# A two-part mixer: nine blocks of 512 tokens in place of sixteen half batches of 288, with TensorE's order written out

## The chip, the cores and the metric

The kernel runs on one core of one Trainium2 chip. The metric is the device time of one execution in microseconds (us). The kernel before takes 811.2 us, the median of three runs (810.45 to 811.35).

## What is computed

The reference has two parts, one behind the other. Chunked attention gives x; a mixer with two pairs of weight matrices follows, one pair across tokens and one across channels.

```python
B, H, S, D = 8, 8, 576, 64                # batches, heads, tokens, width of a head
# attention inside chunks of 64 tokens (9 chunks in each batch and head)
attn = softmax(q_c @ k_c.T / sqrt(D));  out = attn @ v_c
x = out as (B, S, 512)
# the mixer: w_tok1 576x256, w_tok2 256x576, w_ch1 512x1536, w_ch2 1536x512
xt = x.transpose(0, 2, 1)
u  = x + (relu(xt @ w_tok1) @ w_tok2).transpose(0, 2, 1)
out = u + relu(u @ w_ch1) @ w_ch2
```

The weights come as 64-bit floats, which the kernel turns into 32-bit ones itself. The sums over tokens stay inside one batch of 576 tokens. The channel part (the last line) treats each token by itself, so its tokens may be grouped across batches.

## The kernel before, in words

**Attention.** The tokens of the 8 batches are loaded as 36 tiles of 128 (L251, L256): tiles 0 to 4 hold batch 0 and the first 64 tokens of batch 1, tiles 5 to 8 the rest of batch 1, and so on. For a tile TensorE makes scores `s`; VectorE subtracts their maximum (`mx` L282, `pr` L285); ScalarE takes the exponential (L289). The probabilities then have to be transposed. In the first five tiles TensorE does that (L351, "t"); from tile 5 on VectorE transposes 32x32 blocks (L332), the result goes out to DRAM as `far` and comes back rearranged as `pf` (L337, L343), and ScalarE copies it to `pt` (L360). TensorE then makes `v`, VectorE divides into `x` (L400), ScalarE and GpSimd split x into a high part `xh` (L417) and a low part `xl` (L418). A product of two split operands takes three fp32r matmuls (high by high, low by high, high by low). x itself goes out and back through DRAM as `xt`, transposed, for the sum in u.

**Weights.** Each piece is fetched as raw 64-bit words (L139). ScalarE reads it twice (L156, L157), VectorE clamps, shifts, adds the sign and adds the low word (L160, L166, L173, L181), ScalarE rounds a high part (L225) and VectorE subtracts to get the low part (L231). Of the channel weights there are 24 pieces of 512 columns: c1 0 to 11 and c2 0 to 11. `convert(n)` puts the next n of VectorE's steps at a place in the program.

**Token part.** `tok1` (L476) gives for a batch two sums of 14 matmuls, 512 columns wide; `tok2` (L514) uses them for u, 288 tokens (half a batch) at a time. u is split into `uh` and `ul` (L524, L525). Batch 0 takes plain fp32 operands in one term in place of three (L485, L514).

**Channel part.** For a half batch and each of 12 pieces f, `ch1` (L535) does 12 matmuls of 288 columns; `gh` (L544, ScalarE) and `gl` (L545, VectorE) are made of the result; `ch2` (L575) does 12 more into four accumulators. Each ch2 stands one ch1 late, behind the ch1 of the next piece. At the end o is added up and written (L582 to L585).

**What sets the order.** The start (five tiles, tok1 and tok2 of batch 0) is written out by hand on TensorE, ScalarE and VectorE. Then, until batch 1's mixer begins, a scheduler places the instructions of all engines: both halves of batch 0 run through ch1 together, piece by piece, the second half keeps its g (L541) and runs ch2 afterwards, and the four tiles of batch 1 are spread over slots (`STARTS`, `JOBS`); the split of the token weights stands at the end of that (`split`). From batch 1 on TensorE's order is by hand; the other engines' comes from the scheduler. Each engine runs its instructions in its order, and so does SyncE with the DMAs: whoever waits holds up all behind it.

Of the kernel before, what the change touches and what calls it, by code (L numbers as in the profile page):

```python
# [8 lines left out]
F32 = mybir.dt.float32  # L9
# [41 lines left out]
X_BEFORE = ((), (), (0,), (1,), (2,), (3, 4))  # L51

END_FILL = (4, 3, 1)
STEP_FILL = (5, 5)

STARTS = ((8, 9, 11, 12), (13, 14, 16, 17), (18, 19, 21, 22), (23, 24, 26, 27))
STARTS = ((8, 9, 11, 12), (13, 14, 16, 17), (18, 19, 21, 22), (23, 24, 26, 27))
JOBS = [(9, "ready")]
JOBS += [(s, "part", j, k) for j, ss in enumerate(STARTS) for k, s in enumerate(ss)]
JOBS += [(27 + i, "split", i) for i in range(7)]  # L60


@with_exitstack
def attention_mixer_kernel(ctx, tc, qk_in, v_in, w1_in, w2_in, wc1_in, wc2_in, out):

# [36 lines left out]
    plan += [(("t2", k, n), w2_in, k * S + n * HALF, HALF) for n in range(2) for k in range(NT1)]  # L120
# [50 lines left out]
    def words_sign(i):  # L171
        ti = tops[i].bitcast(I32)
        nc.vector.scalar_tensor_tensor(  # L173
            out=ti, in0=raws[i][1][:, :, 1], scalar=-0x40000000, in1=ti,
            op0=ALU.bitwise_and, op1=ALU.bitwise_or,
        )
        raws[i][0].__exit__(None, None, None)
# [41 lines left out]
    def split_high(i):  # L219

        key, _, _, n = plan[i]
        name = "kept_" + "_".join(map(str, key))
        kept = ctx.enter_context(tc.tile_pool(name=name, bufs=1, reuse_waits="tile"))
        parts = tops[key, "parts"] = kept.tile([P, 2, n], F32R, name=name)
        nc.scalar.copy(out=parts[:, 0], in_=tops[i])  # L225
# [21 lines left out]
    xt = const.tile([P, S // BK, NDT, BK], F32, name="xt")  # L247
# [190 lines left out]
    def attn_x(b, i, ps=None):  # L438

        for t, rows, j in mix_tiles(b):  # L440
            if t != i:
                continue
            dst = xt[:, 4 * j:4 * j + (rows.stop - rows.start) // BK]
            if ps is None:
                far_in(tiles[t]["x"], dst, rows)
            else:
                nc.scalar.copy(  # L447
                    out=dst.rearrange("p i n c -> p n i c"),
                    in_=near(tiles[t]["x"], ps).rearrange("p (n q) -> p n q", n=NDT)[:, :, rows]
                    .rearrange("p n (i c) -> p n i c", c=BK),  # L450
                )
# [53 lines left out]
    def tok2(b, r, n, m, dst):  # L505

        uh, ul = dst
        ps = ps_acc.tile([P, 512], F32, tag="acc", name="ps_t2")
        for k in range(NT1):
            terms = [(r[k], tops["t2", k, n])] if b == 0 else [  # L510
                (r[k][ri], weights["t2", k, n][:, wi]) for wi, ri in THREE
            ]
            for q, (lhsT, rhs) in enumerate(terms):
                nc.tensor.matmul(  # L514
                    ps[:, :HALF], lhsT=lhsT[:, m * P:(m + 1) * P], rhs=rhs,
                    start=(k == 0 and q == 0), stop=(k == NT1 - 1 and q == len(terms) - 1),
                )
        u = pool.tile([P, HALF], F32, tag="u", name="u", bufs=4)
        nc.vector.tensor_tensor(  # L519
            out=u.rearrange("p (i c) -> p i c", c=BK),  # L520
            in0=ps[:, :HALF].rearrange("p (i c) -> p i c", c=BK),
            in1=xt[:, n * HALF // BK:(n + 1) * HALF // BK, m], op=ALU.add,
        )
        nc.scalar.copy(out=uh[:, m], in_=u)  # L524
        return lambda engine: engine.tensor_tensor(  # L525
            out=ul[:, m], in0=u, in1=uh[:, m].bitcast(F32), op=ALU.subtract
        )

    def ch1(u, f, kept=False):
        while ("c1", f) not in weights:  # L530
            convert(1)
        ps = ps_c1.tile([P, 512], F32, tag="c1", name="ps_c1")
        for k in range(NDT):
            for q, (wi, ui) in enumerate(THREE):
                nc.tensor.matmul(  # L535
                    ps[:, :HALF], lhsT=weights["c1", f][:, wi, k * P:(k + 1) * P], rhs=u[ui][:, k],
                    start=(k == 0 and q == 0), stop=(k == NDT - 1 and q == 2),
                )
# [11 lines left out]
    def g_parts():  # L550
# [8 lines left out]
    def ch2(b, n, u, f, g, accs):  # L559
# [13 lines left out]
        for e in range(NDT):  # L573
# [5 lines left out]
            if f < NFC - 1:  # L579
                continue  # L580
# [273 lines left out]
```

## Time and profile before

| | |
|---|---|
| median of three runs | 811.2 us |
| span of the profiled execution | 808.2 us |
| TensorE busy | 787.4 us, 97% |
| VectorE busy | 378.0 us, 47% |
| ScalarE busy | 240.7 us, 30% |
| GpSimd busy | 118.5 us, 15% |
| mean granted TensorE clock | 0.992 |

The page gives for the profiled execution its span alone, from the first instruction to the last; the median of the runs is 3.0 us above it, and that difference is what lies around the span. TensorE's share is an average of two stretches: in the first 180 us it is busy for 163.3, and from there until its last matmul it has no idle time that the profile shows. VectorE's 47% is an average too: it is busy for 49.9 of the 50 us from 52 to 102.

### The profile page before, as it was taken

The page shows a single profiled execution, that of the slowest core. Times are in us where ns is not written, and L with a number is a line of the kernel's source. Part 1 is how long each engine was busy: PE and PEld are TensorE (multiplying, and loading weights), DVE is VectorE, ACT ScalarE, POOL GpSimd, SP SyncE. Part 2 cuts the span into 40 slices and gives each one's busy share as a digit, 9 for nine tenths or more (in the row PEclk, how much of TensorE's full clock was granted, in tenths as well). Part 3 has the DMA queues.
Part 4 walks back from the last instruction along what each step waited for, and adds up shares of the span by engine and source line. Part 5 has one row for each costly group of instructions (what it writes and reads, how often), then busy time and mean ns, then how long its engine had stood idle before and what let it go on. Part 6 is the DMA issues. An engine that isn't in the chain of part 4 may idle for free.

```text
span 808.2 us, 17939 instructions
## 1 busy us (share of the span) xinstructions
PE 787.4 (97%) x7556; PEld 752.1 (93%) x7556; DVE 378.0 (47%) x799; ACT 240.7 (30%) x496; POOL 118.5 (15%) x137
## 2 busy tenths in 40 slices
PE   7889999899999999999999999999999999999997
PEld 5579989799999999999999999999999999999997
DVE  5989985545344344253534334344533445232111
ACT  4667643322232222132223222222223222121111
POOL 0000120401203021130203102030200302033000
PEclk8999999999999999999999999999999999999999
DMA  9953322344432233123441234222342223200000
GB/s 349 406 190 105 119 79 96 135 122 141 148 112 64 92 122 107 56 79 125 141 151 58 64 115 140 88 70 93 131 145 89 76 88 101 67 30 1 1 30 30
DMA packets 69985, 87.96 MB, mean 109 GB/s; under 512 B 8016, under 2 KB 48208, under 8 KB 69904
## 3 DMA queue, kind: packets, MB, share of 16 engines
q1 hardware_dynamic: 69904, 86.82, 32.5%
q8 instruction: 59, 0.97, 0.5%
q14 instruction: 22, 0.18, 0.1%
HBM read 59.92 MB, written 25.95 MB: 106 GB/s over the span
## 4 chain that ended last, share of the span: by engine, by line
PE 85%; DVE 8%; DMA 3%; ACT 2%; issue 1%; SPq 0%; ACTq 0%; DVEq 0%
PE acc L575 36%; PE ps_c L535 33%; PE ps_t L476 6%; PE ps_t L514 6%; PE ps_sv L309 2%; PE ps_sv L321 2%; DVE wtop L173 1%; DVE wtop L181 1%; DMA xc<-x 1%; DVE kept_c L231 1%; DVE wtop L160 1%; DMA raw_t<-in_w 1%; DMA pf<-far 1%; DVE wtop L166 1%; PE sum L485 0%
## 5 line engine op out<-in xcount | busy, mean ns | idle before, releaser
L535 PE MATMUL ps_c<-uh,kept_c 128*128 128x288 f32 x1536 | 310.8, 295 | 3.4 <-ACT xt L447 1.9
L575 PE MATMUL acc<-gh,kept_c 128*128 128x288 f32 x1536 | 311.9, 299 | 1.6 <-ACT kept_c L225 1.1
L535 PEld LDWEIGHTS ps_c<-uh,kept_c 128*128 128x128 f32 x1536 | 245.8, 188 | 4.8 <-ACT xt L447 2.1
L575 PEld LDWEIGHTS acc<-gh,kept_c 128*128 128x128 f32 x1536 | 244.2, 188 | 6.4 <-ACT kept_c L225 1.8
L535 PE MATMUL ps_c<-ul,kept_c 128*128 128x288 f32 x768 | 226.6, 295 | 0.0
L545 DVE SCALAR_TENSOR_TENSOR gl<-ps_c,gh 128x288 fp32r<-128x288 f32 x180 | 81.4, 452 | 310.1 <-ACT gh L544 309.9
L575 PE MATMUL acc<-gl,kept_c 128*128 128x288 f32 x768 | 219.5, 295 | 0.0
L544 ACT ACTIVATE gh<-ps_c 128x288 fp32r<-128x288 f32 x180 | 74.1, 411 | 317.1 <-PE ps_c L535 316.6
L535 PEld LDWEIGHTS ps_c<-ul,kept_c 128*128 128x128 f32 x768 | 144.2, 188 | 0.1
L575 PEld LDWEIGHTS acc<-gl,kept_c 128*128 128x128 f32 x768 | 142.9, 189 | 0.1
L418 POOL TENSOR_TENSOR xl<-x,xh 128x512 fp32r<-128x512 f32 x28 | 38.3, 1366 | 413.0 <-ACT xh L417 413.0
L584 POOL TENSOR_TENSOR o<-o,ul 128x288 f32<-128x288 f32 x56 | 44.1, 813 | 192.7 <-DVE o L582 191.1
L514 PE MATMUL ps_t<-kept_t,rh 128*128 128x288 f32 x224 | 44.7, 295 | 0.3 <-ACT rh L493 0.3
L289 ACT ACTIVATE pr<-pr 128x512 f32<-128x512 f32 x36 | 22.7, 632 | 61.6 <-DVE pr L285 59.9
L582 DVE TENSOR_TENSOR o<-acc,uh 128x288 f32<-128x288 f32 x56 | 22.7, 448 | 36.1 <-PE acc L575 31.5
L476 PE MATMUL ps_t<-xh,kept_t 128*128 128x512 f32 x112 | 36.0, 405 | 2.5 <-ACT xh L417 2.5
L524 ACT CAST uh<-u 128x288 fp32r<-128x288 f32 x64 | 27.1, 433 | 37.6 <-DVE u L519 37.6
L360 ACT COPY pt<-pf 128x512 f32<-128x512 f32 x31 | 19.2, 620 | 60.3 <-DMA pf<-far 60.3
L514 PEld LDWEIGHTS ps_t<-kept_t,rh 128*128 128x128 f32 x224 | 35.9, 188 | 1.0 <-ACT rh L493 1.0
L514 PE MATMUL ps_t<-kept_t,rl 128*128 128x288 f32 x112 | 33.2, 297 | 0.2 <-DVE rl L494 0.2
L519 DVE TENSOR_TENSOR u<-ps_t,xt 128x288 f32<-128x288 f32 x64 | 28.4, 452 | 9.8 <-PE ps_t L514 9.4
L525 POOL TENSOR_TENSOR ul<-u,uh 128x288 fp32r<-128x288 f32 x35 | 29.1, 848 | 10.0 <-ACT uh L524 9.5
(79 smaller groups left out, 629.4 us busy)
## 6 DMA issues: line engine op xcount, KB each, us to landing
qk<-in_qk SPq DMA_DIRECT2D x36, 512.0 KB, 3.9
far<-blocks SPq DMA_DIRECT2D x63, 256.0 KB, 2.1
raw_c<-in_wc SPq DMA_DIRECT2D x24, 512.0 KB, 9.0
v<-in_v SPq DMA_DIRECT2D x36, 260.0 KB, 4.1
out<-o SPq DMA_DIRECT2D x64, 144.0 KB, 1.9
pf<-far SPq DMA_DIRECT2D x124, 64.0 KB, 2.0
xt<-far SPq DMA_DIRECT2D x112, 64.0 KB, 2.0
raw_t<-in_w SPq DMA_DIRECT2D x4, 288.0 KB, 7.9
```

The costliest lines, as they stand in the source:

```text
L289: nc.scalar.activation(out=pr, in_=pr, func=AF.Exp, scale=1.0 / float(D) ** 0.5)
L418: nc.gpsimd.tensor_tensor(out=xl, in0=t["x"], in1=xh.bitcast(F32), op=ALU.subtract)
L476: nc.tensor.matmul(ps, lhsT=lhsT, rhs=rhs, start=(n == 0 and q == 0), stop=(n == len(mt) - 1 and q == len(terms) - 1),)
L514: nc.tensor.matmul(ps[:, :HALF], lhsT=lhsT[:, m * P:(m + 1) * P], rhs=rhs, start=(k == 0 and q == 0), stop=(k == NT1 - 1 and q == len(term ...
L519: nc.vector.tensor_tensor(out=u.rearrange("p (i c) -> p i c", c=BK), in0=ps[:, :HALF].rearrange("p (i c) -> p i c", c=BK), in1=xt[:, n * H ...
L524: nc.scalar.copy(out=uh[:, m], in_=u)
L525: return lambda engine: engine.tensor_tensor(out=ul[:, m], in0=u, in1=uh[:, m].bitcast(F32), op=ALU.subtract)
L535: nc.tensor.matmul(ps[:, :HALF], lhsT=weights["c1", f][:, wi, k * P:(k + 1) * P], rhs=u[ui][:, k], start=(k == 0 and q == 0), stop=(k == N ...
L544: nc.scalar.activation(out=gh, in_=ps[:, :HALF], func=AF.Relu)
L545: nc.vector.scalar_tensor_tensor(out=gl, in0=ps[:, :HALF], scalar=0.0, in1=gh.bitcast(F32), op0=ALU.max, op1=ALU.subtract)
L575: nc.tensor.matmul(accs[e], lhsT=weights["c2", f][:, wi, e * P:(e + 1) * P], rhs=g[gi], start=(f == 0 and q == 0), stop=(f == NFC - 1 and ...
L584: nc.gpsimd.tensor_tensor(out=o, in0=o, in1=u[1][:, e].bitcast(F32), op=ALU.add)
```

## The change

All 4608 tokens are taken as one row and cut into nine blocks of 512 for the channel part; the output is laid out to match. `tok2` makes u for a block out of the one or two batches that it touches (64 tokens of block 1 belong to batch 0, 448 to batch 1, and so on). ch1, ch2, g and o are 512 columns wide. Block 0's channel pieces are cut in two: 0 to 7 run first, then all 12 pieces of block 1, then pieces 8 to 11 of block 0, whose partial output waits in DRAM in between (`part`, `back`). `tok2_first` adds x for block 0 by matmuls with the identity in place of the transposes "x" and `xt`. The tiles of batch 1 run at pieces 0, 2, 4 and 6 of block 0 (`SLOTS`), by the one function `attention` that serves the other batches: it makes the scores of one tile and the `v` of the tile before in one go. Raw pieces share 8 buffers and are fetched 7 ahead, where before each had its own and was fetched 6 ahead. All `ul` are made by VectorE, where GpSimd made 35 of 64. TensorE's order is by hand from the start to the end; the order of the others behind the start is the scheduler's.

```diff
+N = 512
+NB = B * S // N
+F0 = 8
+SEGMENTS = [(0, 0, F0), (1, 0, NFC), (0, F0, NFC)] + [(k, 0, NFC) for k in range(2, NB)]
+SLOTS = {
+    (0, 0): (0, 2, 4, 6), (1, 0): (3, 6, 9, 11), (0, F0): (1,),
+    2: (2, 4, 7, 9), 3: (1, 3, 5, 7, 9),
+}
+CONVERT = {(0, 0): 10, (1, 0): 4, (0, F0): 0}
-AHEAD = 6
+AHEAD = 7
+RAW_BUFS = 8
-    plan += [(("t2", k, n), w2_in, k * S + n * HALF, HALF) for n in range(2) for k in range(NT1)]
+    plan += [(("t2", k), w2_in, k * S, S) for k in range(NT1)]
...
+    def tok2_first(r, m, dst, ps):
+        uh, ul = dst
+        cols = slice(m * P, (m + 1) * P)
+        for j in range(N // P):
+            nc.tensor.matmul(
+                ps[:, j * P:(j + 1) * P], lhsT=tiles[j]["x"][:, cols], rhs=ident,
+                start=(j == 0), stop=False,
+            )
+        for k in range(NT1):
+            nc.tensor.matmul(
+                ps, lhsT=r[k][:, cols], rhs=tops["t2", k][:, :N], start=False, stop=(k == NT1 - 1)
+            )
+        nc.scalar.copy(out=uh[:, m], in_=ps)
+        nc.vector.tensor_tensor(out=ul[:, m], in0=ps, in1=uh[:, m].bitcast(F32), op=ALU.subtract)
...
     def ch1(u, f):
-                    ps[:, :HALF], lhsT=weights["c1", f][:, wi, k * P:(k + 1) * P], rhs=u[ui][:, k],
+                    ps, lhsT=weights["c1", f][:, wi, k * P:(k + 1) * P], rhs=u[ui][:, k],
...
+    def split():
+        for i in range(token):
+            split_high(i)
+            split_low(i)
...
+    by_hand.enter_context(tc.manual_schedule(engines={nc.tensor.engine}))
+    done, pend, accs = 0, None, []
+    attention(done)
+    done += 1
+    ready()
+    for seg, (k, lo, hi) in enumerate(SEGMENTS):
+        slots = SLOTS.get((k, lo), SLOTS[3 - (k + 1) % 2] if 2 <= k < B - 1 else ())
+        for f in range(lo, hi):
+            g = ch1(us[k], f)
...
+            convert(CONVERT.get((k, lo), 0))
+            if (k, f) == (0, F0 - 3):
+                split()
+            if f - lo in slots:
+                attention(done)
+                done += 1
+            turn = f == hi - 1 and seg + 1 < len(SEGMENTS) and SEGMENTS[seg + 1][1] == 0
+            if turn:
+                b = SEGMENTS[seg + 1][0]
+                if b < B:
+                    rs[b] = [tok1(b, m) for m in range(NT1)]
+            if pend is not None:
+                ch2(*pend)
+            pend = (k, us[k], f, g, accs)
+            if turn:
+                us[b] = block_u()
+                two = ps_at.tile([P, 2, 512], F32, tag="at", name="ps_t2")
+                for m in range(NDT):
+                    ps = ps_c1.tile([P, N], F32, tag="c1", name="ps_t2") if m < 2 else two[:, m - 2]
+                    tok2(b, rs, m, us[b], ps)
+            if turn or (k, f) == (NB - 1, NFC - 1):
+                ch2(*pend)
+                pend = None
```

Two places in the built order matter below. The first is VectorE in the start, between the second and the third tile. In these rows `mx` and `pr` are the maximum and the difference of a tile's scores, `wtop` a weight piece in conversion, `zi` and `x` the division of the tile before, and `kept` the split weights. Before:

```order
L173 SCALAR_TENSOR_TENSOR wtop_292<-raw_t1_2_2_205,wtop_292 128x512
L166 TENSOR_SCALAR wtop_360<-wtop_360 128x256
L181 ISA wtop_292<-wtop_292,low_293 128x1024
L282 TENSOR_REDUCE mx_425<-ps_s_389 128x8
L160 TENSOR_SCALAR wtop_380<-wtop_380 128x288
L285 TENSOR_TENSOR pr_428<-ps_s_389,mx_425 128x2x4x64
L393 TENSOR_SCALAR zi_431<-ps_v_406 128x8
```

And in the change, where the lines have new numbers (L148 is L173, L141 is L166, L155 is L181, L266 is L282, L135 is L160, L269 is L285, L209 is L231, L377 is L393):

```order
L148 SCALAR_TENSOR_TENSOR wtop_177<-raw_106,wtop_177 128x512
L209 TENSOR_TENSOR kept0_465<-wtop_147,kept0_465 128x512
L141 TENSOR_SCALAR wtop_245<-wtop_245 128x256
L155 ISA wtop_177<-wtop_177,low_178 128x1024
L266 TENSOR_REDUCE mx_311<-ps_s_275 128x8
L135 TENSOR_SCALAR wtop_265<-wtop_265 128x576
L269 TENSOR_TENSOR pr_314<-ps_s_275,mx_311 128x2x4x64
L209 TENSOR_TENSOR kept0_465<-wtop_177,kept0_465 128x512
L377 TENSOR_SCALAR zi_317<-ps_v_292 128x8
```

The scheduler has moved the split of the token weights (`split()`, which the text of the program puts at piece 5 of block 0) into the start: two of its subtractions (L209) stand between a tile's steps here, three more and the two masks (L688) stand a little behind.

The second place is TensorE behind the start, around the `v` of tile 5. Before, the scheduler had put it in small groups among the matmuls of pieces 2 and 3 of both halves (uh_677 and ul_678 are the second half's u):

```order
L535 MATMUL ps_c1_1028<-uh_677,kept_c1_3_861 128x288 x2
L535 MATMUL ps_c1_1028<-ul_678,kept_c1_3_861 128x288
L575 MATMUL acc_903<-gl_933,kept_c2_2_892 128x288
L575 MATMUL acc_904<-gl_933,kept_c2_2_892 128x288
L575 MATMUL acc_905<-gl_933,kept_c2_2_892 128x288
L575 MATMUL acc_906<-gl_933,kept_c2_2_892 128x288
L379 MATMUL ps_v_1260<-v_741,pt_1258 64x65 x7
L575 MATMUL acc_903<-gh_1008,kept_c2_3_972 128x288
```

In the change (ps_sv_603 holds the scores of tile 5, ps_sv_697 those of tile 6 and the `v` of tile 5, ps_c1_654 and ps_c1_766 are ch1 of pieces 0 and 1):

```order
L293 MATMUL ps_sv_603<-qk_514 64x64 x5
L540 MATMUL ps_c1_654<-uh_540,kept0_465 128x512 x2
L540 MATMUL ps_c1_654<-ul_541,kept0_465 128x512
L540 MATMUL ps_c1_654<-uh_540,kept0_465 128x512 x2
L540 MATMUL ps_c1_654<-ul_541,kept0_465 128x512
L540 MATMUL ps_c1_654<-uh_540,kept0_465 128x512 x2
L540 MATMUL ps_c1_654<-ul_541,kept0_465 128x512
L540 MATMUL ps_c1_654<-uh_540,kept0_465 128x512 x2
L540 MATMUL ps_c1_654<-ul_541,kept0_465 128x512
L293 MATMUL ps_sv_697<-qk_597 64x64 x16
L305 MATMUL ps_sv_697<-v_516,pt_695 64x64 x16
L540 MATMUL ps_c1_766<-uh_540,kept0_465 128x512 x2
```

The `v` of tile 5 (L305, which needs `pt`) now stands right behind the first ch1, with nothing but that ch1 between it and the tile's scores, and all later ch1 and ch2 stand behind it.

More of the change, by code (lines that the diff above doesn't have):

```diff
@@ L50 @@
 PREPARE = (0, 2, 2, 2, 2)
[L51 to L60, printed above, removed]
+END_FILL = (4, 3, 2)
 @with_exitstack
@@ L246, in attention_mixer_kernel, with xt @@
     tiles = {}
-    xt = const.tile([P, S // BK, NDT, BK], F32, name="xt")
+    xts = {}
+    def xt(k):
+        if k not in xts:
+            xts[k] = pool.tile([P, N // BK, NDT, BK], F32, tag="xt", name="xt")
+        return xts[k]
     def load_qk(i):
@@ L442, in attn_x @@
                 continue
[L443 to L451, printed above, removed]
+            first, end = (b * S + j * P) // BK, (b * S + j * P + rows.stop - rows.start) // BK
+            while first < end:
+                k, at = divmod(first, N // BK)
+                n = min(end - first, N // BK - at)
+                part = slice(rows.start, rows.start + n * BK)
+                far_in(tiles[t]["x"], xt(k)[:, at:at + n], part)
+                rows = slice(part.stop, rows.stop)
+                first += n
     def batch_tiles(b):
@@ new lines, in tok2 @@
+    def tok2(k, rs, m, dst, ps):
+        uh, ul = dst
+        cols = slice(m * P, (m + 1) * P)
+        tail = k * (S - N)
+        for b, at, n, lo in ((k - 1, 0, tail, S - tail), (k, tail, N - tail, 0)):
+            if not n:
+                continue
+            terms = []
+            for t in range(NT1):
+                if b == 0:
+                    terms.append((rs[b][t], tops["t2", t][:, lo:lo + n]))
+                else:
+                    terms += [(rs[b][t][ri], weights["t2", t][:, wi, lo:lo + n]) for wi, ri in THREE]
@@ L636, in attention_mixer_kernel @@
             tok1_first(j - 1, sums)
+    second = batch_tiles(1)
+    attn_load(second[0])
     convert(END_FILL[0])
@@ L731, in attention_mixer_kernel @@
[L731 to L745 removed]
+    order = [t for b in range(1, B) for t in batch_tiles(b)]
@@ new lines, in ready @@
+    def ready():
+        attn_stack(first[4], range(1, 2))
+        tiles[first[4]]["x"] = far_out(tiles[first[4]]["x"], "far_s")
+        attn_x(0, first[4])
+    def split():
+        for i in range(token):
+            split_high(i)
+            split_low(i)
+        for c in range(2):
+            kept_half = half_kept[:, c]
+            nc.vector.tensor_scalar(
+                out=kept_half, in0=weights["t1", 4][:, 1].bitcast(F32),
+                scalar1=half_mask[:, c:c + 1], scalar2=None, op0=ALU.mult,
+            )
+            half_low.append(kept_half)
```

259 lines of the change are left out of this document (71 added, 188 removed).

## Prediction

> **What bounds the kernel now.** I read the page first.
>
> ```profile
> span 808.2 us, 17939 instructions
> PE   7889999899999999999999999999999999999997
> DVE  5989985545344344253534334344533445232111
> ```
>
> Each digit is a 40th of the span, 20 us. VectorE (DVE) is nearly full in slices 2 to 6 and half empty later; TensorE (PE) is full from slice 10 on. The stages, by the view of windows (busy time of PE, weight loads, DVE, ACT, POOL, then the granted clock):
>
> ```profile
> 20.00:40.00 20.00, 16.74 (x178) 9.95 (x179) 18.28 (x46) 13.14 (x27) 0.00 (x0) 1.00 1.03 407
> 60.00:80.00 20.00, 20.00 (x173) 19.31 (x172) 20.00 (x43) 15.20 (x30) 0.00 (x0) 1.00 0.31 106
> 300.00:400.00 100.00, 100.00 (x1010) 97.42 (x1012) 41.61 (x86) 24.11 (x50) 16.92 (x18) 1.00 0.31 100
> ```
>
> So there are two regimes. Up to about 115 us VectorE has no room (20.00 of 20), because it converts the weights; behind that TensorE alone sets the time. The change touches both. In the second regime the chain of waits gives the prices (start, us, what, count):
>
> ```profile
> 182.07 0.62 PE ps_sv L309 x32
> 182.70 0.47 PE ps_sv L321 x32
> 183.17 1.80 PE acc L575 x12
> 184.96 1.58 PE ps_c L535 x12
> 186.54 1.60 PE acc L575 x12
> ...
> 238.08 3.27 PE ps_t L476 x14
> 241.35 1.59 PE acc L575 x12
> 242.94 3.26 PE ps_t L476 x14
> 246.20 1.59 PE acc L575 x12
> 247.80 6.33 PE ps_t L514 x48
> ```
>
> A 288-column matmul of the channel part costs 3.18/24 = 0.1325 us (a ch1 and a ch2), a 512-column one of tok1 3.26/14 = 0.233, tok2 of a batch 6.33, a tile's attention 0.62 + 0.47 + 0.20 (the ch2 behind it takes 1.80, not 1.60) = 1.29; the tok2-to-tok2 times of whole batches give 1.25, which I use. The two widths give 3.7 ns a matmul and 0.448 ns a column.
>
> **TensorE's work, before and after.** Channel part: 16 x 12 x 24 = 4608 matmuls x 0.1325 = 610.6 before; 9 x 12 x 24 = 2592 x 0.233 = 603.9 now: -6.7. tok2 of the later blocks: 7 x 6.33 = 44.3 before; now the same columns in two unequal pieces for a block, 24 x (512 x 0.448 + 2 x 3.7 ns) = 5.68 for each of k = 2 to 7 and 24 x 0.233 = 5.6 for k = 8, together 39.7, and 6.1 for k = 1 (24 of 448 columns, 4.9, and eight fp32 ones of 64 columns at about 0.15): +1.5. Batch 0's tok2 is plain fp32:
>
> ```profile
> 25.55 1.98 PE L485 MATMUL sum<-x,wtop 128*128 128x512 f32 x4
> 27.38 0.60 PE L351 MATMUL ps_x<-ident,x 128*128 128x128 f32 x4
> 35.49 4.52 PE L514 MATMUL ps_t<-wtop,r 128*128 128x288 f32 x16
> 39.85 1.04 PE L351 MATMUL ps_x<-ident,x 128*128 128x128 f32 x8
> ```
>
> Start to start, two such 512-column matmuls (four records) take 1.83, a half batch of tok2 4.36, and a 128-column transpose about 0.11. Before: 2 x 4.36 + 20 x 0.11 = 10.9. tok2_first: 8 x 0.91 + 16 matmuls of 128 columns by the identity, in fp32 two records each, 16 x 0.22 = 10.8. No gain. tok1 and attention keep their counts. TensorE's work falls by about 5 us, 0.6%; that is all that the wider blocks bring by these rows.
>
> The Trainium skill (TensorE: Matmul & The Clock Gate, Back-to-back issue gap) puts an isolated matmul at N/2.4 + 2.5 ns, so 122.5 ns for 288 columns and 215.8 for 512, and the channel part at 564.5 before and 559.4 after, -5.1 in place of -6.7. The trace disagrees on both widths (132.5 and 233), so the rows are used.
>
> **VectorE's work up to the turn to block 1.** I follow the built order of VectorE to X, the `x` of batch 1's last tile, since tok1 of batch 1 waits for it. Its steps, start to start:
>
> ```profile
> 29.29 0.69 DVE L173 SCALAR_TENSOR_TENSOR wtop<-raw_c,wtop 128x512 int32<-128x512 int32 x1
> 29.89 0.42 DVE L166 TENSOR_SCALAR wtop<-wtop 128x512 int32<-128x512 int32 x1
> 30.23 0.68 DVE L181 CUSTOM_DVE_ANT_0 wtop<-wtop,low 128x1024 uint16<-128x1024 uint16 x1
> 30.83 0.42 DVE L160 TENSOR_SCALAR wtop<-wtop 128x512 f32<-128x512 f32 x1
> 31.17 0.68 DVE L173 SCALAR_TENSOR_TENSOR wtop<-raw_c,wtop 128x512 int32<-128x512 int32 x1
> ```
>
> 0.60 for a 512-column step with two tensors (a maximum or a sum too), 0.34 for one with a scalar. A 512-column piece costs 3 x 0.60 + 2 x 0.335 = 2.47. In the change, ahead of and with X, there stand 25 pieces (23 of the channel weights) 61.8; the smaller token pieces and the masks 7.5; mx and pr of ten tiles 12.0; nine x 5.4; zi of five 1.6; two transposes and the sum of four 8.6; seven gl and four ul 6.6; r, the stack and the memset 1.4: 104.8 us. The same count for before, up to its last conversion, is 98.4. There VectorE waited as well:
>
> ```profile
> 5.69 0.69 DVE L282 TENSOR_REDUCE mx<-ps_s 128x8 f32<-128x512 f32 x1 [4.67 <-PE ps_s L270]
> 10.04 0.43 DVE L160 TENSOR_SCALAR wtop<-wtop 128x512 f32<-128x512 f32 x1 [2.26 <-ACT wtop L156]
> 35.60 0.69 DVE L643 TENSOR_SCALAR r<-sum 128x512 f32<-128x512 f32 x1 [0.54 <-PE sum L485]
> 114.05 0.69 DVE L231 TENSOR_TENSOR kept_c<-wtop,kept_c 128x512 fp32r<-128x512 f32 x1 [1.00 <-ACT kept_c L225]
> ```
>
> The last conversion is done at 114.65, so its waits were 114.65 - 98.4 = 16.3; up to r they were 35.6 - 26.1 of work = 9.5. The change keeps the first two waits. Its work up to r is 33.1, 7.0 more (token splits 3.4, channel pieces further ahead), so r comes about 7 us later and with it block 0's u; work there that is done early comes off later, so only the sum to X counts. I take before's 16.3 for the waits, with 9.5 (none behind the start) and 22 as ends: in the change `kept0` in the start waits behind ScalarE's copies, and conversions of pieces 20 on wait for raw loads behind `far` on SyncE. To that comes GpSimd:
>
> ```profile
> 84.01 2.99 POOL L418 TENSOR_TENSOR xl<-x,xh 128x512 fp32r<-128x512 f32 x1 [82.48 <-ACT xh L417]
> 129.15 1.28 POOL L418 TENSOR_TENSOR xl<-x,xh 128x512 fp32r<-128x512 f32 x1 [8.85 <-ACT xh L417]
> 85.86 1.42 DVE L160 TENSOR_SCALAR wtop<-wtop 128x512 f32<-128x512 f32 x1
> ```
>
> An xl takes 2.99 beside a full VectorE and 1.28 beside a free one, and VectorE loses 1.0 (1.42 for 0.41). There are three xl ahead of X where before had two: +1.0. **X at 104.8 + 16.3 + 1.0 = 122.1.**
>
> **From X to the end.** xh 0.6 (as a 512-column step), xl 2.1 (between 1.28 and 2.99), then on TensorE what waits for it: the last matmul of tok1's first sum and its second sum, 15 x 0.233 = 3.5; ch2 of piece 6, 2.8; tok2 of block 1, 6.1; ch2 of piece 7, 2.8. Block 1 begins at 140.0. From there TensorE has 100 pieces (8 blocks and 4 pieces of block 0) x 24 x 0.233 = 559.2, six tok1 39.1, tok2 39.7, 27 attention steps, the last one half, 33.3: 671.3. At the turns VectorE needs u, then ScalarE's copy, then ul for each quarter, about 2.0 us against 1.5 of tok2; by the fourth it is 2 us behind, which ch2 of piece 11 (2.8) and the first nine matmuls of the next ch1 hide. The tail:
>
> ```profile
> 803.86 0.29 PE L575 MATMUL acc<-gl,kept_c 128*128 128x288 f32 x1
> ```
>
> 4.05 from the end of the last matmul to 808.2; 4.5 with 512 columns. Sum: 140.0 + 671.3 + 4.5 = 815.8 for the span against 808.2, and with the 3.0 around it **818.8 us** against 811.2: slower by 0.9%.
>
> TensorE inside the first stretch: the `v` of tile 5 now stands behind one ch1, and what it needs takes, with idle engines,
>
> ```profile
> 158.51 0.69 PE L309 MATMUL ps_sv<-qk 64*64 64x64 f32 x32
> 161.54 0.71 DVE L332 STREAM_TRANSPOSE blocks<-pr 128x512 f32<-128x512 f32 x1 [0.70 <-ACT pr L289]
> 164.37 1.75 SPq L343 DMA_DIRECT2D pf<-far  x4
> 168.47 0.70 PE L321 MATMUL ps_sv<-v,pt 64*64 64x64 f32 x32 [0.49 <-ACT pt L360]
> ```
>
> 10 us from scores to `v`. TensorE has 2.8 of work in that time, so it stands for at least 7 us behind the first ch1, more like 11 with VectorE's queue, and a few us at each later slot (two pieces, 11.2 us, apart). I cost this at nothing because VectorE runs on meanwhile: block 0's 8 pieces, tok1, tok2 and the slots are 60 us of TensorE between about 57 and 140.
>
> **The rivals.** (1) VectorE never waits behind the start. For it: the longer stretch gives TensorE's work more time to be ready, and slots two pieces apart leave it a queue of conversions. Against it: the first two waits alone are 6.9 us, and new copies stand in its way in the start. With 7.8 to 9.5 us of waits in all (9.5 is before's up to r) the median is 810.3 to 812.0, not slower; it decides from 8.7 us of waits down, which is par (16.3 less the 7.6 of the sum). About 811: 0.16. (2) 512-column matmuls are cheaper in ch1 and ch2 than in tok1. Each ns is 2.4 us, so at 0.229 the median is 809.2, and every further ns takes 2.4 off. For it: the fp32 records above come nearer to it. Against it: tok1's rows are the same kind of matmul at the same width. 0.12, of which 0.03 for a fall by more than 10 ns. The Trainium skill's 215.8 ns, named above, would make it 41 us less (778); tok1's rows speak against it. (3) The TensorE stalls don't stay in VectorE's shadow: raw pieces take
>
> ```profile
> raw_c<-in_wc SPq DMA_DIRECT2D x24, 512.0 KB, 9.0
> ```
>
> 9.0 to landing and stand behind `far` on SyncE. If VectorE waits twice for 3.5 us of that, it is 7 us more: 826. 0.20. (4) The turns are not hidden, 1 to 2 us at each of 8: about 831. 0.04.
>
> **The numbers.** My forecast (waits from 11 to 20 us) has 0.48. A measurement of this kernel tells 0.2% (1.6 us) from no change: faster is under 809.6, slower over 812.8. Faster: 0.06 of rival 1 (with a matmul a little cheaper) and rival 2's 0.12: 0.18. Same: 0.10 of rival 1 and 0.02 of the forecast: 0.12. Slower: the rest of the forecast and rivals 3 and 4, 0.70. The range goes from waits of 9.5 with 0.231 a matmul (818.8 - 6.8 - 4.8 = 807) to waits of 22 with 0.234 (818.8 + 5.7 + 2.4 = 827).
>
> **What would show it.** A ch1 or ch2 of 12 in 2.80; block 1's first ch1 near 140 (under 132: the change is no loss); VectorE above 95% from 45 to 120; TensorE idle about 10 us behind the first ch1; r near 43; no idle TensorE after 140. If the steady stages are as priced and block 1 begins before 130, the step that failed is VectorE's waits.

## The result, and the profile after

The changed kernel takes 834.1 us (median of 4 runs, 832.9 to 837.4), the kernel before 811.3 beside it: a ratio of 1.0292, 95% interval 1.0267 to 1.0317. The sign of the forecast was right and its size wrong: +23 us where +7.6 was forecast, above the upper end of 827.0. The profiled execution has a span of 831.2 us, 2.9 below the median.

First the page of the changed kernel (busy tenths in 40ths of the span, here 20.8 us, and the granted clock of TensorE):

```profile
span 831.2 us, 13454 instructions
PE   6685679999999999999999999999999999999997
DVE  4979786423534433454443435534442323115112
PEclk7696799999999999999999999999999999999999
```

Against before, TensorE is emptier in slices 1 to 6 (but for the third), and in four of these six its clock is lower too. From slice 7 on all looks as it did. The same stretches in the view of windows (PE, weight loads, DVE, ACT, POOL, clock, DMA share, GB/s), with one more:

```profile
20.00:40.00 20.00, 12.07 (x181) 7.51 (x181) 18.99 (x43) 12.73 (x24) 0.00 (x0) 0.71 0.65 238
60.00:80.00 20.00, 9.28 (x90) 7.49 (x90) 19.58 (x39) 11.05 (x20) 0.00 (x0) 0.66 0.39 124
80.00:100.00 20.00, 12.46 (x103) 9.90 (x102) 14.29 (x27) 9.50 (x18) 2.41 (x2) 0.74 0.52 174
300.00:400.00 100.00, 99.22 (x806) 81.83 (x805) 43.88 (x76) 22.70 (x38) 13.31 (x10) 1.00 0.37 118
```

From 60 to 80 us TensorE works 9.28 us where it worked 20.00 before; from 80 to 100 VectorE, too, has 5.7 us of idle time. So the two engines wait for each other, in turns. The chain of waits through that stretch (start, us, what):

```profile
70.13 2.36 DMA far<-blocks
...
74.45 4.06 DMA raw<-in_wc
78.58 0.67 ACT wtop L131
...
83.70 0.63 DVE blocks L316
84.34 2.48 DMA far<-blocks
...
88.73 2.12 DMA far<-blocks
...
92.98 3.99 DMA raw<-in_wc
...
106.11 2.10 DMA far<-blocks
...
111.18 3.75 DMA raw<-in_wc
114.95 0.67 ACT wtop L131
...
117.26 0.63 DVE blocks L316
117.91 4.32 DMA far<-blocks
...
123.64 2.06 DMA pf<-far
125.80 0.63 ACT pt L344
126.47 0.69 PE ps_sv L305 x32
127.16 4.53 PE acc L568 x12
131.69 2.72 PE ps_c L540 x12
134.41 6.45 PE ps_t L459 x28
140.87 2.72 PE acc L568 x12
143.59 5.01 PE ps_t L522 x30
...
149.37 1.93 PE ps_t L522 x10
151.30 2.72 PE acc L568 x12
```

This is a ring, gone round every 18.4 us (74.45, 92.98, 111.18): a raw weight load on SyncE, ScalarE's copy of it, VectorE's conversions, behind those in VectorE's order a tile's transposes, the tile's transfers on SyncE, and behind these in SyncE's order the next raw loads. TensorE hangs on it by the `v` of each tile. At the last slot the chain goes over `v` itself, and the ch2 behind it takes 4.53 us where 12 such matmuls take 2.72 elsewhere: after a stand TensorE's clock is at half (granted 0.50 from 92 to 96 us, behind the second). From that `v` on the chain stays on TensorE up to block 1, but for a wait of 0.8 us in tok2: ch2, ch1, tok1 (L459), ch2, tok2 (L522), ch2. It doesn't pass through the last x of batch 1. The waits of TensorE, then those of VectorE, in that stretch (us in all, times, longest):

```profile
PE ps_sv L305 <- ACT pt L344: 22.8, 4, 8.8
```

```profile
DVE wtop L135 <- ACT wtop L131: 5.8, 4, 2.6
DVE ul L505 <- ACT uh L504: 2.5, 1, 2.5
DVE mx L266 <- PE ps_sv L305: 2.3, 1, 2.3
```

Four stands of 8.8, 7.5, 2.7 and 3.9 us. VectorE's rows, for r and for the last x of batch 1, and ScalarE's just behind that:

```profile
44.82 0.69 DVE L642 TENSOR_SCALAR r<-sum 128x512 f32<-128x512 f32 x1 [0.87 <-PE sum L468]
...
130.12 0.68 DVE L384 TENSOR_TENSOR x<-ps_sv,zs 128x512 f32<-128x512 f32 x1
```

```profile
133.31 0.66 ACT L131 ACTIVATE wtop<-raw 128x512 f32<-128x512 f32 x1 [2.44 <-DMA raw<-in_wc]
133.88 0.67 ACT L132 ACTIVATE low<-raw 128x512 int32<-128x512 uint32 x1
134.44 0.62 ACT L401 CAST xh<-x 128x512 fp32r<-128x512 f32 x1
```

The x ends at 130.80. Of that time VectorE was at work 106.9 us and idle 23.9 (the gaps over 0.12 us between its rows, added up; 11.6 of them ahead of r). Its xh is made only 3.6 us later, since ScalarE has two copies of a raw piece ahead of it and waits for their load. That costs TensorE nothing here: the last xl is done at 136.8, and the first matmul that reads it starts at 137.25, right behind the one before. Block 1's first ch1 starts at 153.9.

The steady part, in the chain of waits again, with the turn to block 2 and the first ch1 of blocks 2 and 3:

```profile
164.90 2.72 PE acc L568 x12
...
242.55 6.45 PE ps_t L459 x28
...
262.94 5.44 PE ps_c L540 x24
...
347.38 5.44 PE ps_c L540 x24
```

Twelve 512-column matmuls of ch1 or ch2 take 2.72 (0.2267 each), tok1 of a batch 6.45, block 2 as a whole 84.4. The tok2 between them (TensorE's rows; two 128-column and two 384-column groups in a quarter, then the wait ahead of the last quarter):

```profile
251.85 0.38 PE L522 MATMUL ps_t<-kept,rh 128*128 128x128 f32 x2
252.07 0.28 PE L522 MATMUL ps_t<-kept,rl 128*128 128x128 f32 x1
252.19 0.57 PE L522 MATMUL ps_t<-kept,rh 128*128 128x384 f32 x2
...
256.55 0.33 PE L522 MATMUL ps_t<-kept,rl 128*128 128x384 f32 x1
258.19 0.44 PE L522 MATMUL ps_t<-kept,rh 128*128 128x128 f32 x2 [1.30 <-DVE u L527]
```

A 128-column matmul takes 0.11 us (251.85 to 252.07 for two), twice what its columns ask for, and the fourth quarter starts 1.64 after the last matmul of the third. This tok2 takes 8.45 us where 5.68 was forecast.

### The profile page after: what moved, and what is told of

The parts are those of the page before. It is cut to its first block, busy times and chain, and to the rows that moved or that the text cites. A ratio compares the mean times of both kernels' runs of the same rounds, so it can differ in the third digit from the quotient of the medians.

```text
span 831.2 us, 13454 instructions
## 1 busy us (share of the span) xinstructions
PE 780.8 (94%) x5552; PEld 633.7 (76%) x5552; DVE 374.7 (45%) x660; ACT 214.1 (26%) x361; POOL 86.1 (10%) x74
## 4 chain that ended last, share of the span: by engine, by line
PE 82%; DMA 7%; DVE 5%; ACT 2%; SPq 1%; issue 1%; ACTq 0%; DVEq 0%
PE acc L568 35%; PE ps_c L540 33%; PE ps_t L522 6%; PE ps_t L459 5%; DMA raw<-in_wc 2%; PE ps_sv L293 2%; PE ps_sv L305 2%; DMA far<-blocks 2%; DMA qk<-in_qk 2%; DMA raw<-in_w 1%; SPq L327 1%; DVE u L527 1%; DVE wtop L148 1%; ACT wtop L131 1%; ACT low L132 1%
## 5 line engine op out<-in xcount | busy, mean ns | idle before, releaser
L568 PE MATMUL acc<-gh,kept 128*128 128x512 f32 x864 | 274.8, 400 | 0.0
L540 PE MATMUL ps_c<-uh,kept 128*128 128x512 f32 x864 | 267.8, 391 | 0.0
L546 DVE SCALAR_TENSOR_TENSOR gl<-ps_c,gh 128x512 fp32r<-128x512 f32 x108 | 74.5, 690 | 335.7 <-ACT gh L545 326.1
L540 PEld LDWEIGHTS ps_c<-uh,kept 128*128 128x128 f32 x864 | 162.9, 189 | 34.8
L568 PEld LDWEIGHTS acc<-gh,kept 128*128 128x128 f32 x864 | 161.9, 190 | 34.9
L568 PE MATMUL acc<-gl,kept 128*128 128x512 f32 x432 | 170.7, 395 | 0.0
L540 PE MATMUL ps_c<-ul,kept 128*128 128x512 f32 x432 | 168.8, 391 | 0.3 <-DVE ul L505 0.3
L545 ACT ACTIVATE gh<-ps_c 128x512 fp32r<-128x512 f32 x108 | 64.5, 597 | 316.6 <-PE ps_c L540 314.3
L568 PEld LDWEIGHTS acc<-gl,kept 128*128 128x128 f32 x432 | 82.4, 191 | 18.2
L540 PEld LDWEIGHTS ps_c<-ul,kept 128*128 128x128 f32 x432 | 81.4, 188 | 17.8 <-DVE ul L505 0.8
L522 PE MATMUL ps_t<-kept,rh 128*128 128x448 f32 (+7 forms) x224 | 49.6, 314 | 6.2 <-DVE u L527 6.2
L522 PEld LDWEIGHTS ps_t<-kept,rh 128*128 128x128 f32 x224 | 37.1, 189 | 9.3 <-DVE u L527 7.9
L305 PE MATMUL ps_sv<-v,pt 64*64 64x64 f32 x992 | 21.2, 225 | 22.8 <-ACT pt L344 22.8
L305 PEld LDWEIGHTS ps_sv<-v,pt 64*64 64x64 f32 x992 | 18.2, 140 | 23.8 <-ACT pt L344 23.4
L459 PE MATMUL ps_t<-xh,kept 128*128 128x512 f32 x112 | 34.9, 393 | 0.0
L522 PE MATMUL ps_t<-kept,rl 128*128 128x448 f32 (+7 forms) x112 | 34.7, 311 | 0.0
```

Of the source, the lines that this page charges most:

```text
L305: nc.tensor.matmul(ps[c * CH:(c + 1) * CH, a, (NHP + hp) * D:(NHP + hp + 1) * D], lhsT=t["pt"][a * CH:(a + 1) * CH, hp, c * CH:(c + 1) * C ...
L459: nc.tensor.matmul(ps, lhsT=lhsT, rhs=rhs, start=(n == 0 and q == 0), stop=(n == len(mt) - 1 and q == len(terms) - 1),)
L522: nc.tensor.matmul(ps[:, at:at + n], lhsT=lhsT[:, cols], rhs=rhs, start=(q == 0), stop=(q == len(terms) - 1),)
L540: nc.tensor.matmul(ps, lhsT=weights["c1", f][:, wi, k * P:(k + 1) * P], rhs=u[ui][:, k], start=(k == 0 and q == 0), stop=(k == NDT - 1 and ...
L545: nc.scalar.activation(out=gh, in_=ps, func=AF.Relu)
L546: nc.vector.scalar_tensor_tensor(out=gl, in0=ps, scalar=0.0, in1=gh.bitcast(F32), op0=ALU.max, op1=ALU.subtract)
```

## The experiments

Four theories are told apart. **A**: the ring through SyncE, in which the raw loads are the late part, sets block 1's start. **B**: TensorE's stands for `v` set it. **C**: VectorE's work up to the last x of batch 1 sets it. **D**, formed after the twelfth run: no single one does, since several chains of nearly the same length run side by side. The turn's wait is a question by itself (e4). Times are medians, with the kernel before on the same chip, the ratio's 95% interval, and from the traces, of one execution each, the end of the last x of batch 1 and the start of block 1's first ch1:

| run | us | before | ratio | x | block 1 |
|---|---|---|---|---|---|
| the change | 834.1 | 811.3 | 1.0267 to 1.0317 | 130.8 | 153.9 |
| e1 | 831.2 | 810.4 | 1.0215 to 1.0286 | 127.2 | 151.5 |
| e2 | 841.4 | 810.4 | 1.0341 to 1.0428 | 137.0 | 159.9 |
| e3 | 830.6 | 810.4 | 1.0201 to 1.0347 | 128.6 | 150.8 |
| e4 | 825.3 | 810.4 | 1.0145 to 1.0213 | 131.7 | 153.8 |
| e5 | 835.5 | 811.5 | 1.0281 to 1.0335 | 125.0 | 154.8 |
| e6 | 827.6 | 811.5 | 1.0185 to 1.0240 | 126.4 | 149.7 |
| e7 | 825.4 | 811.5 | 1.0157 to 1.0196 | 123.5 | 147.0 |
| e8 | 821.3 | 811.5 | 1.0100 to 1.0145 | 126.2 | 150.3 |
| e9 | 823.6 | 809.9 | 1.0140 to 1.0180 | 123.5 | 147.1 |
| e10 | 825.0 | 809.9 | 1.0158 to 1.0206 | 130.6 | 153.9 |
| e11 | 817.0 | 809.9 | 1.0062 to 1.0104 | 126.3 | 145.5 |
| e12 | 821.4 | 809.9 | 1.0115 to 1.0157 | 122.4 | 144.4 |
| e13 | 807.9 | 811.1 | 0.9938 to 0.9987 | 110.5 | 131.8 |
| e14 | 826.0 | 811.1 | 1.0169 to 1.0210 | 134.1 | 154.8 |
| e15 | 820.1 | 811.1 | 1.0095 to 1.0138 | 126.1 | 148.3 |
| e16 | 839.8 | 811.1 | 1.0335 to 1.0379 | 141.4 | 163.3 |
| e17 | 827.8 | 811.5 | 1.0178 to 1.0224 | 136.1 | 156.6 |
| e18 | 819.3 | 811.5 | 1.0075 to 1.0111 | 128.0 | 148.9 |

**The turn (e4).**

```
-                two = ps_at.tile([P, 2, 512], F32, tag="at", name="ps_t2")
...
-                    ps = ps_c1.tile([P, N], F32, tag="c1", name="ps_t2") if m < 2 else two[:, m - 2]
+                    ps = ps_c1.tile([P, N], F32, tag="c1", name="ps_t2")
```

> All four quarters of tok2 go into the two PSUM buffers of ch1, in place of the first two there and the last two in one buffer of two banks. If the wait ahead of the last quarter (1.06 to 1.64 us at eight turns, 9.5 in all, less 0.2 each for a matmul) comes from that shared buffer, it goes: 8 us less, 826, and block 1 begins 1 us earlier. If VectorE's u, ScalarE's copy and ul take too long in any case (the turn's chain, 2.0 us a quarter), the wait comes back ahead of a quarter or ahead of the next ch1: 832 to 835. The matmuls of 64 to 192 columns should stay at 111 ns.

Waits of TensorE behind 140 us, of the changed kernel and then of e4, the only ones each view names:

```profile
PE ps_t L522 <- DVE u L527: 7.0, 8, 1.3
```

```profile
PE ps_t L459 <- DVE stack L418: 1.0, 1, 1.0
```

As expected: the wait is gone, 8.8 us less, and block 1 starts where it did. So the wait came from the two last quarters sharing one tile: the matmuls of the last one wait until `u` of the third has been read. Whether the chip asks for this wait or the program's bookkeeping by tiles does, no run tells. The small matmuls keep their 0.11 us (tok2 of block 2 is 6.88 now, not 5.68).

**One cause at a time (e1 to e3), on the changed kernel.**

```
-AHEAD = 7
-RAW_BUFS = 8
+AHEAD = 10
+RAW_BUFS = 11
```

> Three more raw buffers, the raw weight loads issued three pieces earlier (10 ahead in place of 7); nothing else is touched. Theory A (the ring through SyncE: a raw load stands there behind the four transfers of the tile before it, ScalarE and VectorE wait for it, and the next tile's transposes stand behind those conversions): of VectorE's 10.3 us of waits for ScalarE's copies most go, x of batch 1's last tile comes by about 123 in place of 130.1, block 1's first ch1 near 146 in place of 153.9, the time 825 to 829 in place of 834. Rival B (TensorE itself holds everything up, because it stands 22.8 us at the four slots for a tile's v): raw loads have nothing to do with it, 832 to 836.

VectorE's waits for raw copies behind 36 us fell from 7.0 to 2.8, but block 1 came only 2.4 earlier. All 29 pieces now stand ahead of the x (28 in the change), and TensorE still stands 20.7 us at the slots. A's size is not met.

```
-            nc.sync.dma_start(
+            queue = nc.gpsimd if i >= 20 else nc.sync
+            queue.dma_start(
```

> The last nine raw weight loads (pieces 20 to 28) are issued by GpSimd's queue in place of SyncE's; buffers and order as they were. Theory A: as with more raw buffers, SyncE's ring is cut at three of its four rounds, 826 to 830, with block 1 near 147. Rival B: 832 to 836. If the loads land early and VectorE still waits, the ring is closed elsewhere.

In the chain of waits of e2:

```profile
79.35 9.59 DMA raw<-in_wc
```

Slower than the change. GpSimd issued its loads early, from 62 to 80 us, but pieces 18 and 19, which stayed on SyncE and are needed first, then took 7.5 and 9.6 us to land beside them where 4.1 and 5.3 had been enough. ScalarE and VectorE waited for these, so the run doesn't test A as it was meant to. Why r was 2.5 later as well stays open.

```
-    (0, 0): (0, 2, 4, 6), (1, 0): (3, 6, 9, 11), (0, F0): (1,),
+    (0, 0): (1, 3, 5, 6), (1, 0): (3, 6, 9, 11), (0, F0): (1,),
```

> Attention steps of block 0's first segment behind the ch1 of pieces 1, 3, 5, 6 in place of 0, 2, 4, 6, so that a tile's v has one ch1 and one ch2 more ahead of it at the first three. Rival B (TensorE's stand at the slots, 8.8 + 7.5 + 2.7 + 3.9 us and about 2 us of half-speed matmuls behind each, sets block 1's start): 5 to 10 us less, 824 to 829. Theory A (the raw loads' ring sets it): the stands get shorter, but the last x comes as late or later, since the steps begin later: 832 to 838.

TensorE's stands hardly changed (21.9 in place of 22.8), and block 1 came 3.1 earlier: neither theory as put. The tile's `v` still starts at 71.3, because its `pt` isn't there sooner.

**Less of VectorE's work ahead of the x (e5 to e8).** All have the first edit, e6 to e8 also that of e4; e7 has the slots of e3 and one more raw buffer, e8 the three more of e1.

```
-CONVERT = {(0, 0): 10, (1, 0): 4, (0, F0): 0}
+CONVERT = {(0, 0): 5, (1, 0): 6, (0, F0): 0}
```

> Half as many conversion steps for each piece of block 0's first segment (5 in place of 10), and 6 in place of 4 in block 1: nothing is left out, but 23 pieces of weights in place of 28 are done on VectorE when x of batch 1's last tile stands there. Theory C (VectorE's work up to that x, 106.9 us of it and 23.9 us of waits, sets block 1's start): 5 pieces x 2.47 us less, 12.3, so the x ends near 118 in place of 130.8 and block 1 begins near 141: 820 to 823 in place of 834. Theory A (raw loads behind the transfers): the wait of 2.6 us for the last four raw pieces goes as well, 818 to 821. Rival B (TensorE's stands of about 23 us at the slots set it): the stands stay and block 1 begins near 152, 831 to 834.

> The smaller number of conversion steps (5, 6) and tok2's four quarters in ch1's two buffers together. If the two are independent: 8.8 us below the smaller number alone, 811 to 814, about level with the kernel before; with rival B 822 to 826.

> As the last one, with the slots behind pieces 1, 3, 5, 6 and one more raw buffer (8 ahead); 25 pieces stand ahead of the last x in place of 23. Theory C: two more pieces cost 5 us, less 2 of waits, 813 to 817. Rival B: the later slots shorten TensorE's stands, 806 to 810.

> As the sixth, with three more raw buffers (10 ahead): raw loads come early, but the scheduler then also puts 26 pieces ahead of the last x in place of 23. Theory C: 7.4 us more work, less the 3 to 5 us of waits for raw loads: 814 to 818. Theory A: the waits decide, 808 to 811.

None of the four times falls into a range of any theory. C fails: in e5 VectorE had 13.1 us less work up to the x (93.8) and 7.4 us more waits (31.3). The raw loads follow the conversion steps in the program, so with fewer steps ahead of each slot fewer loads stand ahead of its transfers. The waits moved to the turn, where e5's tok2 of block 1 took 13.1 us (one row for ScalarE, one for TensorE):

```profile
ACT wtop L131 <- DMA raw<-in_wc: 19.8, 5, 6.2
...
PE ps_t L522 <- DVE u L527: 4.2, 1, 4.2
```

In e6 and e7 block 1 starts 4 to 7 us earlier than in e4, and is 6 us longer (114.5 and 115.0 in place of 108.7): given back, at its first ch1 in e6, which waits for `ul` behind the late conversions. e8, where the loads come early as well, is the only one that kept its gain, 4 us on e4.

**Parts left out (e9 to e13), on e4.** These leave work or data out, so that one chain at a time is cut. e9 converts pieces 18 to 28 from piece 17's raw words and loads none of them; e10 uses earlier pieces' weights for the last seven; e11 multiplies v by a constant for four tiles.

```
+            if i >= 18:
+                raws[i] = raws[17, 0]
+                continue
```

> On top of the tok2 edit (825.3): the eleven raw weight loads that stand behind the first transfers of the segment are left out; pieces 18 to 28 are converted in full, but from the raw words of piece 17. All the work of every engine stays, only the DMA loads and the waits for them go, and one piece more (29) stands ahead of batch 1's last x. Theory A (ring through SyncE): VectorE's waits for raw loads (7.5 us between 44 and 131) and ScalarE's ahead of xh (about 2.5) go: 816 to 820. Theory C (VectorE's work up to the x): 824 to 828, since there is a piece more. Rival B (TensorE's stands at the slots): 824 to 826. The combination, work and loads taking turns as the bound: 820 to 823.

```
+            if i >= 24:
...
+                    weights[plan[i][0]] = weights[plan[i - 8][0]]
...
-            if i < len(plan):
+            if i < 22:
                 prepare(i + 1 - len(prepared))
```

> On top of the tok2 edit (825.3): the raw loads stay where they are in SyncE's order, but the conversion of the last seven pieces on ScalarE and VectorE is left out, so 22 pieces stand ahead of the last x in place of 28 (their matmuls use the weights of earlier pieces). Theory C: 6 x 2.47 = 14.8 us off VectorE ahead of the x, 810 to 813. Theory A: only the ring counts, which still goes round as often: 820 to 825. Rival B: 824 to 826.

```
-                            lhsT=t["pt"][a * CH:(a + 1) * CH, hp, c * CH:(c + 1) * CH],
+                            lhsT=ident[a * CH:(a + 1) * CH, c * CH:(c + 1) * CH] if j in order[:4]
+                            else t["pt"][a * CH:(a + 1) * CH, hp, c * CH:(c + 1) * CH],
```

> On top of the tok2 edit (825.3): the v matmuls of the first four tiles behind the start read a constant in place of pt, so TensorE doesn't stand at the slots for the round trip of the probabilities; transfers, copies and all other work stay as they are. Rival B: the 24 us of stands and about 8 us of half-speed matmuls behind them go, block 1 begins near 130, 800 to 806. Theory A and C: what sets the last x is SyncE's ring and VectorE's order, and TensorE waits for weights or for x in place of pt: 820 to 825.

e12 has the edits of e9 and e10.

> Both: no late raw loads and no conversion of the last seven pieces, on top of the tok2 edit (825.3). If work and loads take turns as the bound, only this one gives the whole: x near 115, block 1 near 137, 806 to 811, more than the sum of the two before it. If TensorE's stands are the bound (B): 822 to 826.

e13 has all three.

> On top of the tok2 edit (825.3, block 1's first ch1 at 153.8): no late raw loads, no conversion of the last seven pieces, and v of the first four tiles not waiting for pt, all at once. Taken out one by one they gave block 1 at 147.1, 153.9 and 145.5, two together 144.4. If several chains of nearly the same length run side by side (theory D), this one falls to what TensorE's own work asks for: 56.5 + about 61 us of work + tok2's and the first waits, block 1 near 125 to 132, 802 to 808. If a fourth thing holds it (the qk loads, which stand in SyncE's order behind the transfers of the tile before), TensorE waits ahead of the scores instead: block 1 at 140 to 145, 814 to 818.

No theory's gain came in the run that was to show it: A has 816 to 820 for e9 (823.6), C 810 to 813 for e10 (825.0), B 800 to 806 for e11 (817.0), and work and loads in turns 806 to 811 for e12 (821.4). In e10 VectorE has 14.6 us less work up to the x and waits 13.5 us longer (38.2 for e4's 24.7). Block 1 comes earlier by 6.7 us without the loads, not at all without the work, by 8.3 without v's wait, by 9.4 without loads and work, and by 22.0 with all three out, where the single ones add up to 15.0. This is D, with e13 at 807.9 and block 1 at 131.8 as it has them: each cut lets the next chain take over. In e9 VectorE is full where it was idle before (windows), so there its work binds:

```profile
80.00:100.00 20.00, 14.58 (x114) 11.59 (x113) 20.00 (x42) 12.46 (x22) 4.47 (x2) 0.83 0.31 107
```

In e11 TensorE stands for the next tile's qk in place of pt:

```profile
PE ps_sv L293 <- DMA qk<-in_qk: 16.6, 3, 8.8
```

And in e13 TensorE is full from 80 us on, as in the kernel before:

```profile
60.00:80.00 20.00, 13.06 (x165) 10.62 (x164) 20.00 (x40) 12.72 (x23) 2.46 (x1) 0.83 0.34 107
80.00:100.00 20.00, 20.00 (x150) 16.11 (x143) 18.52 (x38) 11.81 (x22) 1.29 (x1) 0.91 0.42 133
```

Some kernels with repeated weights give a part back later: from block 1's start to the end e9 takes 674.4, e12 674.8 and e13 672.5 against 670.7 in e4, at 231.6, 231.8 and 230.6 ns a 512-column matmul of ch1 and ch2 in place of 229.3 (mean of the later blocks, from start to start). e10, which repeats weights too, doesn't (669.3, 229.3). Why is open, so block 1's start is their measure.

**With nothing left out (e14 to e18).** All on e4. e14 and e15 send x's transfers of four tiles over ScalarE's queue, e15 with the slots of e3:

```
-        nc.sync.dma_start(out=far, in_=blocks)
+        (queue or nc.sync).dma_start(out=far, in_=blocks)
...
+            tiles[i]["x"], "far_s" if i % NTILE == 4 else "far", nc.scalar if i in order[:4] else None
```

> On top of the tok2 edit (825.3): the transfers of x of the first four tiles (far, then four issues into xt) go through ScalarE's queue in place of SyncE's, so that raw, qk and v loads stand only behind the transfers of pr; nothing is left out. If SyncE's order is the ring, raw loads come about 5 us earlier in each round: block 1 near 148, 818 to 821. If the ring only moves to ScalarE, which now waits for the landing of far (2 to 4 us) ahead of its copies: 824 to 830.

> As the last one, with the slots behind pieces 1, 3, 5, 6. If the effects add (the slots alone gave 3.1 us of block 1's start): 815 to 818. If TensorE's stand for pt is only moved: as the last one.

e14 only moved the ring: ScalarE now waits for transfers ahead of its copies, and v's stands are 25.4 us. With the later slots it is 6 us faster, more than slots alone gave: D again.

e16 cuts block 0 later:

```
-F0 = 8
+F0 = 10
```

> On top of the tok2 edit (825.3): block 0's first segment ends behind piece 9 in place of 7 (two pieces are put behind block 1 in place of four), slots behind 0, 2, 5, 8. TensorE has 10.9 us more work in the stretch where it stands, and the last slot comes later. If the stands between the slots are set by chains that run on meanwhile (theory D), the third slot's and fourth slot's stands (3.4 and 4.6 us) vanish under it and block 1 begins 3 to 6 us later with 10.9 us less to do afterwards: 817 to 821. If block 1's start is a chain of ring rounds and pieces, the work is simply put ahead: 824 to 827.

Block 1 starts 9.5 later with 10.9 us more done, so the two pieces were put ahead for a gain of 1.4 us. The time as a whole, outside both ranges, says nothing of the cut: with two pieces in the segment behind block 1, its one slot fell on the last piece, and tok1 of block 2 stood for it:

```profile
PE ps_t L459 <- DVE stack L418: 13.9, 1, 13.9
```

e17 and e18 put v one slot later, by order alone (8 and 7 conversion steps, e18 with e1's raw buffers):

```
+LAG = (0, 1, 3, 5, 7)
...
+                i = order[n + 1] if n < 4 else None
+                j = order[n - 1] if n else None
+                attn_both(i, j)
```

> Nothing left out: the tok2 edit, and in block 0's first segment a tile's v one slot later than before (scores of tile n beside v of tile n-2, slots 0, 1, 3, 5, 7), so that TensorE has one more round of ch1 and ch2 ahead of each v; 8 and 6 conversion steps a piece, 25 pieces ahead of the last x. If the ring is what the three-fold run shows (TensorE's wait for pt, the raw loads, the conversions), taking v's wait out by order gives at least what the constant in place of pt gave: block 1 at 136 to 146, 808 to 817. If the ring only closes over SyncE's order (v and qk loads, now behind two slots), block 1 stays near 150: 820 to 824.

> As the last one, with three more raw buffers (10 ahead) and 7 conversion steps; 28 pieces ahead of the last x. If raw loads still bind there: 3 to 7 us less than the last one. If VectorE's work binds (3 pieces more, 7.4 us): 0 to 7 us more than the last one.

e17 lies above both its ranges. TensorE now stands at the second slot for the scores, 16.2 us in e17 and 14.5 in e18. In e17 the view names a step of VectorE, in e18 the load, and SyncE's row shows when it was issued, behind all the transfers of the tile before:

```profile
PE ps_sv L294 <- DMA qk<-in_qk: 14.9, 2, 14.5
```

```profile
75.83 0.38 SPq L236 DMA_DIRECT2D qk<-in_qk  x1
```

So v's wait alone isn't it: SyncE's order closes the ring a second way. Raw loads three pieces earlier, with one conversion step less, take 8.5 us off e17, which was expected to be 3 to 7. e18, at 1.0093, and e15 are the best kernels that leave nothing out; none beats the kernel before.

## Why the prediction was wrong

By its own steps, against the 818.8:

- **VectorE's waits up to X** (16.3, taken over from before) is the first term of its sum that failed: 23.9, +7.6. 2.1 of it lies ahead of r. Behind r it waited 12.3, of which 5.8 for copies of raw words; with the late raw loads left out (e9) its waits up to X are 16.3, in place of e4's 24.7. VectorE's work was right (104.8 + 1.0 forecast, 106.9).
- **"I cost this at nothing because VectorE runs on meanwhile"**, of TensorE's stands, is the step that failed as a mechanism: the stands lie on the path to block 1. The forecast left TensorE 83 us from the first ch1 to block 1, 60 of them work. Measured are 97.5 (56.4 to 153.9): 71.6 busy, some 8 of it from the halved clock, and 25.9 idle, 22.8 of that for `v`. And VectorE doesn't run on: its conversions need raw loads that stand in SyncE's order behind transfers of an x, which needs the `v` for which TensorE stands. This is rival 3's mechanism at more than its 7 us: e13, which also leaves work out, took 22.0 us off block 1's start. The rival priced one wait; it should have followed the ring once round. The Trainium skill (DMA: Bandwidth & Descriptors, Anatomy of one DMA) says that a semaphore wait is done on the issuing sequencer, ahead of dispatch; the raw loads at 74.45, 92.98 and 111.18, each right behind the xt issues, agree.
- **From X to block 1** 17.9 forecast, 23.1 measured: +5.2. The forecast has TensorE wait there for xh and xl, and it didn't: it came to the matmul that reads the last xl 0.5 us after that was ready. So X doesn't carry the chain, though it is nearly as long. From the last `v` (126.47) on it is TensorE's own work, with a ch2 of 4.53 for 2.8 and a tok2 of 7.7 for 6.1. In figures, X's 8.7 and this 5.2 make the 13.9 by which block 1 is late.
- **tok2 priced by its columns**: 39.7 forecast for the seven later blocks, 52.7 measured, +13.0. Two terms were missed. Seven waits ahead of the last quarter, 7.9 us (without them, in e4, the seven take 44.8): rival 4's place, but not its mechanism, since the shared tile is at fault and no cover behind it helps (e4). And a floor of 0.11 us below some 250 columns (0.111 us by 0.448 ns a column), the other 5.1 us: the columns 64, 128 and 192 all cost it, as the row of 128 shows. The Trainium skill (TensorE: Matmul & The Clock Gate, LDWEIGHTS) puts a weight load at P/1.2 ns, where P is its columns, not its rows: 106.7 ns for 128, by this estimate. The trace's 111 from start to start is near it. That the load makes the floor is argued and not shown: no run varies it, and the trace's own rows of these loads, which overlap, are 0.19 us long.
- **The price of a 512-column matmul**, taken from tok1 (0.233): 2.72/12 = 0.2267 in ch1 and ch2. With what the matmuls behind attention steps cost, the channel part took 552.2 for 559.2, -7.0: rival 2 came true in kind, and was covered by the rest.
- Attention came to 29.0 for 33.3 (-4.3), tok1 to 38.7 for 39.1, the tail to 4.6 for 4.5.

818.8 + 13.9 + 13.0 - 7.0 - 4.3 - 0.4 + 0.1 = 834.1. That the steady part, as a whole, was right to 1.5 us (677.3 for 675.8) is luck: tok2's +13.0 nearly cancels with the channel part and attention. Of what was to show it: TensorE's idle time behind the first ch1 (8.8 + 2.3) and r (44.8 for 43) came as said; VectorE above 95% from 45 to 120 did not (62.3 of 75 us, 83%), and this was the sign to read.

What stays open: how much of block 1's 153.9 belongs to which chain (they don't add), what the 512-token blocks would do with TensorE's order in that stretch left to the scheduler, as before (no run has that), and whether an order of SyncE's loads and transfers exists with which the 512-token blocks win. Only a kernel with work left out (e13) went below the kernel before.

## What to carry to other kernels

Where a slot's chain goes through four engines and two of them also feed the next slot, price the whole ring, once round, and don't let one engine's stand vanish behind another's work before it is clear what that work waits for. Cutting one link of such a ring shows the next one; cut several at once to see what there is to gain. Two quarters that share a tile waited for each other here: give each its own buffer, and price short matmuls by a row of their own width, not by their columns.

## What the runs showed of the hardware

In tok2, where each matmul has a load of 128 x 128 weights of its own, one of 64, 128 or 192 columns starts 111 ns after the last (median of the changed kernel), one of 256 119, one of 320 147, of 384 175, of 448 204. After each of the stands, ch1 or ch2 matmuls ran at 0.43 us in place of 0.227 for 3 to 4 us; behind the stand of 2.7 us this began only 1.4 us after its end (109.98 to 113.2). The Trainium skill (TensorE: Matmul & The Clock Gate, Part 1: The HAM clock gate) has half the clock after an idle window of about 3.4 us and as long a time to come back; the size agrees. The 2.7 us stand lies between two groups of 64x64 matmuls, 3.9 us in all without a full-width one, and it isn't shown that the stand alone was enough. Nor does its length decide: in e4 a stand of 2.57 us at the same slot left the granted clock at 1.00 (109.4 to 115), while behind one of 2.35 in e15 and one of 2.47 in e1 it fell (0.55 from 108.2 to 112, and 0.66 from 107 to 112). All four stands of the changed kernel together cost about 8 us this way (what the rounds of 12 and the `v` behind them take beyond their usual time), on top of their 22.8.
